# An mLSTM cell and a two-layer block on one core: states of head pairs in place of head trios, transfers in longer rows, and another order for the first third

## The chip, the cores and the metric

The kernel runs on one core of a Trainium2 chip. The metric is the time of one execution on the device in microseconds (us). All four compute engines of the core take part: TensorE (PE in the profile, with its weight loads as PEld), VectorE (DVE), ScalarE (ACT) and GpSimd (POOL); SyncE (SP) issues transfers.

## The reference

```python
# q, k, v, o_gate: (4, 8, 768, 40) float32; i_gate, f_gate: (4, 8, 768) float32
for t in range(S):                       # per batch and head, D = 40
    m_new = np.maximum(f_gate[:, :, t] + m, i_gate[:, :, t])
    f_stab = np.exp(f_gate[:, :, t] + m - m_new)
    i_stab = np.exp(i_gate[:, :, t] - m_new)
    m = m_new
    C = f_stab * C + i_stab * outer(v_t, k_t)
    n = f_stab * n + i_stab * k_t
    y[:, :, t] = sigmoid(o_t) * (C @ q_t) / np.maximum(np.abs(n . q_t), 1.0)
x = y.transpose(0, 2, 1, 3).reshape(4 * 768, 8 * 40)      # 3072 tokens x 320
h = x @ w_in                             # w_in 320 x 2048, w_out 2048 x 320, float64 in memory
out = (h - np.tanh(h)) @ w_out
```

## The kernel before

**Units.** The sequence is cut into chunks of 128 tokens. One unit is one chunk of one batch with its 8 heads: 24 units, numbered n = 4 * chunk + batch. For a unit the kernel makes the scores of all heads (tile ps: k and q with features on the partitions, tiles kz and qz), masks them to the past (P), and multiplies them by the scaled values (vs) into ph. From the second chunk on it adds to ph what the state of the earlier chunks gives (`inter`: state times q, from a second copy of q, tile q2). It then gates (`gate`, five VectorE instructions), transposes the result into xT (`turn`, `keep_x`), and brings the state on (`update` into pc, `keep_state`). Two units form a group of 256 tokens; there are 12.

**Heads.** kz and qz hold even heads on partitions 0 to 39 and odd heads on 64 to 103, so that two heads' score products stand in different rows of the array. The state holds the heads in trios, with the 40 features of three heads on 120 partitions (`TOP`): trio 0 is heads 0 to 2, trio 1 heads 3 to 5, and trio 2 heads 6 and 7. A state is block-diagonal; the factor eT, zero where a row belongs to another head of the trio, makes it so. `inter` and `update` are thus three matmuls each per unit, two of 123 columns and one of 82.

**The two-layer block.** The 2048 features are 8 pairs p of 2 x 128. For a group and a pair, `up` makes ph_up (from xT and w_in), ScalarE and VectorE make g = h - tanh(h) by a polynomial, and a down product adds it to the output. Groups 0 to 3 and group 11 use direct products (`down`, bank po); groups 4 to 10 use seven products in place of eight (`down_seven`, banks pS). A polynomial's bound is tested at the end, and a general branch, not taken with these inputs, follows.

**Weights.** They arrive as float64 and are taken apart by integer operations: 640 columns a block, two blocks (w_in, w_out) a pair. A block takes five VectorE instructions (`parts` two, `one`, `sign`, `product`) and two on ScalarE. All weight transfers are issued by GpSimd, five for w_in and two for w_out per pair.

**What sets the order.** All instructions of an engine run in the order in which the program adds them. For the first part of the kernel (units 0 to 11 and groups 0 to 3) a list scheduler, class `Plan`, makes that order at build time: an operation has an engine, an assumed duration, predecessors, a rank and tokens for the buffers that it holds, and `run` always emits the one that can start first. The assumed durations decide the order only; on the chip the engines wait for each other by semaphores. Where the plan sees TensorE idle, `idle` puts in some products of ones, 512 columns wide (tile awake, from diag). After that the units 12 to 23 are spread evenly over the block's items by hand (`cell_slot`, `merge`).

**Loads.** `load_unit` loads a unit's tiles: kz, qz and q2 by rows of 512 bytes (one head's 128 tokens), v, k and o by token (1,280 bytes; k 1,440, since a trio's end is filled from the next head). At the start SP loads the gates, then kz and o of units 0 and 1; ACT's queue loads their qz, GpSimd their v and then the weights.

Of the kernel before, what the change touches and what calls it, by code (L numbers as in the profile page):

```python
# [78 lines left out]
def kernel(  # L79
# [77 lines left out]
    class Plan:  # L157
# [5 lines left out]
        RATE, SHARED = 0.25, 32.4  # L163

        def __init__(self, **tokens):
            self.tokens = {name: [(0.0, tag) for tag in (range(tags) if isinstance(tags, int) else tags)] for name, tags in tokens.items()}
            self.turns = {name: 0 for name, tags in tokens.items() if isinstance(tags, int)}
            self.count = tokens
            self.todo, self.free, self.serial, self.moved = [], dict.fromkeys("TVASGN", 0.0), 0, dict(S=8.0, G=6.5)
# [21 lines left out]
        def run(self, idle):  # L191
            while self.todo:
# [12 lines left out]
                op["end"] = self.free[op["engine"]] = t + op["us"]  # L205
# [77 lines left out]
    TRIO = 3  # L283
    TOP = TRIO * D
    WIDE = -(-H // TRIO) * TRIO
    TRIOS = [range(h, min(h + TRIO, H)) for h in range(0, H, TRIO)]

    ld = {}

    def load_unit(n, names=("kz", "qz", "v", "k", "o", "q2"), queue=nc.sync):  # L290
        c, b = divmod(n, B)
        t = ld.setdefault(n, {})
        for name in names:
            if name in ("kz", "qz"):
                t[name] = load.tile([128, HH, L], FP, name=name, tag=name, bufs=3)
                for i in range(2):
                    src = kT if name == "kz" else qT
                    queue.dma_start(out=t[name][i * HALF:i * HALF + D], in_=src[b, c, :, slice(i, H, 2)])
            elif name == "k":
                if n + B < NU:  # L300
                    t["k"] = load.tile([L, WIDE, D], FP, name="k", tag="k", bufs=3)
                    queue.dma_start(out=t["k"].rearrange("p h d -> p (h d)"),
                                    in_=bass.AP(k.tensor, k[b, c].offset, [[H * D, L], [1, WIDE * D]]))
            elif name != "q2":
                src, bufs = {"v": (v, 3), "o": (o_gate, 4)}[name]
                t[name] = load.tile([L, H, D], FP, name=name, tag=name, bufs=bufs)
                queue.dma_start(out=t[name], in_=src[b, c])
            elif c:
                t["q2"] = load.tile([TOP, len(TRIOS), L], FP, name="q2", tag="q2", bufs=3)
                for i in range(TRIO):  # L310
                    queue.dma_start(out=t["q2"][i * D:(i + 1) * D, 0:len(range(i, H, TRIO))], in_=qT[b, c, :, slice(i, H, TRIO)])

# [28 lines left out]
    eT = const.tile([TOP, NU, H], FP, name="eT")  # L341
# [49 lines left out]
    def gate_columns(c0, c1, bank):  # L391
# [28 lines left out]
        def whole():  # L420
            got["whole"] = sums_of(1, ones).rearrange("p c (b h) -> p (c b) h", h=H)
# [8 lines left out]
        def states():  # L430
            for i in reversed(range(TRIO)):
                rows, heads = slice(0, (i + 1) * D), slice(i, H, TRIO)
                A.activation(out=eT[rows, us, heads], in_=got["whole"][rows, :, heads], func=AF.Exp)
                if i:
                    A.mul(out=eT[0:i * D, us, heads], in_=eT[0:i * D, us, heads], mul=0.0)
# [11 lines left out]
    def weights(dst, srcs, queue):  # L447
# [5 lines left out]
        def fetch():  # L453
# [3 lines left out]
            for rows, cols, part in srcs:  # L457
                queue.dma_start(out=to[rows, cols], in_=part)  # L458
# [32 lines left out]
    def blocks_of(p):  # L491
# [4 lines left out]
        every, whole = slice(0, 128), [(slice(0, 128), slices(0, 2), moe_w_in[0:128, slices(2 * p, 2)])]  # L496
        for i in range(2):
            full, half = (FROM[2], FROM[1]), (FROM[1], FROM[2] + HALF)
            whole.append((every, slices(2 + i, 1), moe_w_in[full[i]:full[i] + 128, slices(2 * p + i, 1)]))
# [3 lines left out]
                        [(every, slice(i * DM, (i + 1) * DM), moe_w_out[slices(2 * p + i, 1), :]) for i in range(2)], nc.gpsimd))  # L503
# [4 lines left out]
    state = [[const.tile([TOP, H, D1], FP, name=f"state{b}_{i}") for i in range(2)] for b in range(B)]  # L508
# [3 lines left out]
    def trio(t, j):  # L512

        return t[:, TRIOS[j].start:TRIOS[j].stop].rearrange("p h d -> p (h d)")

# [61 lines left out]
    def inter(n, j):  # L577
# [3 lines left out]
        if t["c"]:  # L581
            rows = slice(0, len(TRIOS[j]) * D)
            T.matmul(trio(t["ph"], j), t["qs"][rows, j, :], trio(state[t["b"]][t["c"] % 2][rows], j), start=(j == 0), stop=False,
                     skip_group_check=True)

    def intra(n, h):
        t = un[n]
        T.matmul(t["ph"][:, h, :], t["P"][:, h % 2, h // 2, :], t["vs"][:, h, :], start=(t["c"] == 0 and h == 0), stop=True,
# [14 lines left out]
    def update(n, j, at_once=True):  # L603
        t = un[n]
        if j == 0:
            t["pc"] = small([TOP, H, D1], "pc")
        T.matmul(trio(t["pc"], j), t["k"][:, TRIO * j:TRIO * (j + 1)].rearrange("p h d -> p (h d)"), trio(t.get("vs_end", t["vs"]), j), start=True, stop=True)
        if j == len(TRIOS) - 1 and at_once:
            keep_state(n)

    def keep_state(n):
        t = un[n]
        old, new = (state[t["b"]][(t["c"] + i) % 2] for i in range(2))
        pc = t["pc"]
        decay = eT[:, n].unsqueeze(2).to_broadcast([TOP, H, D1])
# [16 lines left out]
    def cell_slot(s, o):  # L632
# [11 lines left out]
        for d, heads in enumerate(TRIOS):  # L644
            steps.append((0.22 if o >= B else 0.0, lambda d=d: inter(o, d)))
            steps += [(0.22, lambda h=h: intra(o, h)) for h in heads]
        steps.append((0.0, lambda: gate(o)))
        steps += 5 * pause
        if o + B < NU:
            steps += [(0.2, lambda j=j: update(o, j)) for j in range(len(TRIOS))] + 4 * pause  # L650
# [97 lines left out]
    def up(some, shrink):  # L748
# [4 lines left out]
        def product(i, x, j):  # L753
# [3 lines left out]
            if j < NK:  # L757
                lhs, rhs = w_in[:, p, (2 * j + i) * 128:(2 * j + i + 1) * 128], xT[g % NX][:, at, :]
# [170 lines left out]
    def plan_unit(n, rank):  # L929
# [10 lines left out]
        if n < 2:  # L940
            times = ((6.1, 3.6, 9.0), (7.6, 5.6, 10.5))[n]
            for name, at in zip(("qz", "v", "o"), times):
                u[name] = plan.add("N", 0.0, (lambda: arrive(n)) if name == "qz" else (lambda: None), at=at - 1.7)
        else:
            load("kz", 1.5, 164, (n - 3, "scores"))
            load("qz", 1.5, 164, (n - 3, "scores"))
# [15 lines left out]
        u["scores"] = plan.add("T", 1.35, first_part, [u["qz"]], rank, [("a", held), ("P", held)])  # L962
        u["mask"] = [plan.add("V", 0.68, lambda i=i: ready[1][i](), [u["scores"]], rank, give=[("a", held)] if i else ())
                     for i in range(2)]
        before = of(n - B, "state")
        u["prep"] = plan.add("V", 0.47, lambda: prepare(n, whole=False), [u["v"], u["scores"], *of_tokens[c]], rank, [("vs", held)])
# [4 lines left out]
        def second_part(j):  # L971
            banks[:] = [held["small"]]
            inter(n, j)
            for h in TRIOS[j]:
                intra(n, h)

        for j, heads in enumerate(TRIOS):
            op = plan.add("T", 0.145 * len(heads) + (0.14 if c else 0.0), lambda j=j: second_part(j), [op] if op else [*u["mask"], u["prep"], u["column"], *before, *of(n, "q2") * (c > 0)], rank,
                          take=() if op else [("small", held)], give=[("P", held)] if j == len(TRIOS) - 1 else ())
        u["second"] = op  # L980
        u["gate"] = plan.add("V", 1.5, lambda: gate(n), [op, u["open"], *of(n - 2, "turn")], rank, give=[("small", held)])
# [3 lines left out]
        def updates():  # L985
            banks[:] = [held_c["small"]]
            for j in range(len(TRIOS)):
# [16 lines left out]
    def plan_weights(p, rank, at):  # L1004
        for k, block in enumerate(blocks_of(p)):
            fetch, parts, low, power, one, sign, product = block
            held, r, buffer = {}, rank + 0.36 * k, "w64" + "ab"[k]
            op = plan.add("S" if k else "G", 1.5 if k else 2.8, fetch, (), r, [(buffer, held)], at=(13.0 if p else 6.0) if k else at, kb=655)
            op = plan.add("V", 1.0, parts, [op], r, [("w", held)])
            two = [plan.add("A", 0.74, step, [op], r) for step in (low, power)]  # L1010
            op = plan.add("V", 0.82, one, two[:1], r)
            op = plan.add("V", 0.82, sign, [op, two[1]], r, give=[(buffer, held)])
            converted[p, k] = plan.add("V", 0.82, product, [op] + (of_tokens[NT - 1] + of_states[NT - 1] if p >= KEPT else []), r, give=[("w", held)])
# [81 lines left out]
    def idle(t0, t1):  # L1095


        n = int((t1 - t0) * 0.9 / 0.43 if t0 < 6.0 else (t1 - t0) * 0.4 / 0.215)
# [90 lines left out]
    def begin_any(n):  # L1189
# [3 lines left out]
        for i in range(2):  # L1193
            spread(t["P"][:, i], f_rows, n, slice(i, H, 2))
# [4 lines left out]
        if t["c"]:  # L1199
            t["qs"] = att.tile([128, len(TRIOS), L], FP, name="qs", tag="P", bufs=4)[0:TOP]  # L1200
            for i in range(TRIO):
                spread(t["qs"][i * D:(i + 1) * D, 0:len(range(i, H, TRIO))], g_rows, n, slice(i, H, TRIO))
            for j, heads in enumerate(TRIOS):
                rows = slice(0, len(heads) * D)
                V.tensor_tensor(out=t["qs"][rows, j], in0=t["qs"][rows, j], in1=t["q2"][rows, j], op=OP.mult)

    def keep_any(n):
# [3 lines left out]
        decay = eT[:, n].unsqueeze(2).to_broadcast([TOP, H, D1])  # L1211

        own = att.tile([TOP, H, D1], FP, name="own", tag="P", bufs=4)
        V.memset(own, 1.0)
        for i in range(TRIO):
            heads = slice(i, H, TRIO)
            pattern = [[0, len(range(i, H, TRIO))], [0, D1]]
            if i:
                V.memset(own[0:i * D, heads], 0.0)
            if i < TRIO - 1:  # L1220
                G.affine_select(out=own[:, heads], in_=own[:, heads], compare_op=OP.is_ge, fill=0.0, base=(i + 1) * D - 1,
                                pattern=pattern, channel_multiplier=-1)
# [32 lines left out]
    with tc.If(nc.values_load(again, min_val=0, max_val=128,  # L1255
# [18 lines left out]
        for g in range(NG):  # L1274
            for n in range(g * GT, (g + 1) * GT):
# [6 lines left out]
                for j in range(len(TRIOS)):  # L1282
# [4 lines left out]
                if n + B < NU:  # L1287
                    for j in range(len(TRIOS)):
# [61 lines left out]
```

## Time and profile before

| | |
|---|---|
| median of 3 runs | 556.2 us (555.52 to 556.96) |
| the profiled execution's own time | 555.52 us |
| its span in the profile | 553.7 us |
| PE busy | 539.0 us (97%) |
| DVE busy | 345.7 us (62%) |
| ACT busy | 179.8 us (32%) |
| POOL busy | 34.2 us (6%) |
| moved by DMA | 37.97 MB in 39,818 packets |

The 1.8 us between the span and the time of that execution lie outside the span. A PE that is busy may be busy with products of ones, or with products that run at half rate; the tables of single instructions tell that apart.

### The profile page before, as it was taken

What the parts mean: (1) busy time and instruction counts of PE and PEld (TensorE: products, weight loads), DVE (VectorE), ACT (ScalarE), POOL (GpSimd) and SP (SyncE); (2) the same over time, 40 slices, a digit from 0 to 9 for tenths busy, and PEclk for the clock granted to TensorE, in tenths of its full rate; (3) what the DMA queues carried; (4) which work ended last, traced back from release to release, by engine and by line L of the source; (5) the groups of instructions that cost most, each with busy time, mean ns of one, the idle gap of its engine ahead of it and who ended that gap; (6) DMA issues with size and microseconds to landing.
All of it is one profiled execution on the core that took longest, in us unless ns stands there. A gap on an engine that the chain in (4) does not pass through costs nothing.

```text
span 553.7 us, 8979 instructions
## 1 busy us (share of the span) xinstructions
PE 539.0 (97%) x3378; PEld 455.6 (82%) x3380; DVE 345.7 (62%) x754; ACT 179.8 (32%) x447; POOL 34.2 (6%) x67
## 2 busy tenths in 40 slices
PE   6999999999999999999999999999999999999995
PEld 4768878787877776798899999999989989988873
DVE  4699888989754335767656647547547547553421
ACT  2444653442432312222232242232233233232331
POOL 6042020320000000000000000000000000000000
PEclk9999999999999999999999999999999999999998
DMA  7789345470310001201202212112110000000000
GB/s 217 203 264 255 113 132 156 155 197 23 95 29 0 1 0 49 83 22 55 85 26 60 62 41 69 47 37 60 49 37 12 1 25 1 1 25 1 24 1 30
DMA packets 39818, 37.97 MB, mean 69 GB/s; under 512 B 3992, under 2 KB 37336, under 8 KB 39768
## 3 DMA queue, kind: packets, MB, share of 16 engines
q1 hardware_dynamic: 32336, 22.24, 14.2%
q0 software_dynamic: 3296, 10.82, 6.4%
q10 hardware_dynamic: 4136, 4.26, 2.2%
q8 instruction: 29, 0.48, 0.4%
q14 instruction: 21, 0.17, 0.1%
HBM read 33.37 MB, written 3.93 MB: 67 GB/s over the span
## 4 chain that ended last, share of the span: by engine, by line
PE 91%; DMA 4%; DVE 3%; issue 1%; SPq 0%; ACT 0%; POOL 0%; DVEq 0%; ACTq 0%
PE ph_up L129 38%; PE pS L129 20%; PE po L129 15%; PE ph L129 9%; PE ps L129 4%; PE pc L129 2%; PE px L133 2%; DMA v<-in_v 1%; DMA kz<-in_kT 1%; DMA q<-in_qT 1%; DVE P L106 1%; DVE w_e L106 1%; DMA w<-in_moe_w_in 0%; DVE gt L106 0%; DVE state L106 0%
## 5 line engine op out<-in xcount | busy, mean ns | idle before, releaser
L129 PE MATMUL ph_up<-xT,w_in 128*128 128x256 f32 (+1 forms) x1152 | 245.4, 391 | 2.1 <-DVE w_in L106 1.3
L129 PEld LDWEIGHTS ph_up<-xT,w_in 128*128 128x128 f32 (+1 forms) x1152 | 169.8, 189 | 35.1 <-issue 12.7
L106 ACT ACTIVATE z<-ph_up 128x512 f32<-128x512 f32 (+1 forms) x100 | 57.1, 576 | 284.2 <-issue 160.6
L106 DVE SCALAR_TENSOR_TENSOR gt<-ph_up,z 128x512 f32<-128x512 f32 (+1 forms) x100 | 63.3, 662 | 93.1 <-ACT z L106 92.9
L129 PE MATMUL po<-w_out,gt 128*128 128x320 f32 x320 | 94.4, 440 | 0.0
L129 PEld LDWEIGHTS po<-w_out,gt 128*128 128x128 f32 x320 | 58.4, 190 | 26.4 <-issue 5.0
L106 DVE TENSOR_TENSOR P<-ps,upto 128x512 f32<-128x512 f32 x48 | 31.5, 683 | 68.2 <-PE ps L129 68.2
L129 PEld LDWEIGHTS ph<-vs,P 128*128 128x128 f32 x384 | 60.1, 202 | 5.7 <-issue 1.5
L106 ACT ACTIVATE q<-z,tiny 128x512 f32<-128x512 f32 (+1 forms) x100 | 64.7, 700 | 0.0
L106 DVE SCALAR_TENSOR_TENSOR gt<-q,gt 128x512 f32<-128x512 f32 (+1 forms) x100 | 63.1, 661 | 1.3 <-ACT q L106 1.3
L129 PE MATMUL ph<-vs,P 128*128 128x41 f32 x384 | 58.9, 273 | 0.0
L129 PE MATMUL pS<-wT,s 128*128 128x160 f32 x336 | 51.3, 300 | 0.0
L129 PEld LDWEIGHTS pS<-wT,s 128*128 128x128 f32 x336 | 47.3, 190 | 0.0
L129 PE MATMUL pS<-w_out,gt 128*128 128x160 f32 x224 | 40.4, 310 | 0.0
L129 PEld LDWEIGHTS pS<-w_out,gt 128*128 128x128 f32 x224 | 32.7, 194 | 1.3 <-issue 1.0
L129 PE MATMUL ps<-qz,kz 40*128 40x128 f32 x384 | 29.6, 291 | 1.7 <-DMA kz<-in_kT 1.5
L129 PEld LDWEIGHTS ps<-qz,kz 40*128 40x128 f32 x384 | 26.9, 199 | 5.0 <-DMA qz<-in_qT 1.8
L458 POOL DMA_DIRECT2D w<-in_moe_w_in x40 | 22.2, 561 | 53.3 <-DVE w_e L106 45.1
L129 PE MATMUL ph<-state,q 120*128 120x123 f32 (+1 forms) x120 | 24.3, 284 | 0.0
L106 ACT COPY xT<-px 128x384 f32<-128x384 f32 x24 | 11.4, 475 | 35.6 <-PE px L133 35.6
L129 PEld LDWEIGHTS ph<-state,q 120*128 120x128 f32 (+1 forms) x120 | 19.9, 191 | 1.5
L106 DVE TENSOR_TENSOR s<-gt 128x256 f32<-128x256 f32 x56 | 21.1, 417 | 0.0
(90 smaller groups left out, 441.0 us busy)
## 6 DMA issues: line engine op xcount, KB each, us to landing
w<-in_moe_w_out POOLq DMA_DIRECT2D x16, 320.0 KB, 5.0
kz<-in_kT SPq DMA_DIRECT2D x48, 80.0 KB
o<-in_o_gate SPq DMA_DIRECT2D x24, 160.0 KB
out<-ob ACTq DMA_DIRECT2D x24, 160.0 KB
k<-in_k SPq DMA_DIRECT2D x20, 180.0 KB
qz<-in_qT SPq DMA_DIRECT2D x44, 80.0 KB
v<-in_v SPq DMA_DIRECT2D x22, 160.0 KB
q<-in_qT SPq DMA_DIRECT2D x40, 60.0 KB
```

Source lines behind the costliest of these rows:

```text
L106: i = method(*args, **kwargs)
L129: return cls.keep(nc.tensor.matmul(*args, **kwargs))
L133: return cls.keep(nc.tensor.transpose(*args, **kwargs))
L458: queue.dma_start(out=to[rows, cols], in_=part)
```

## The change

It has five parts.

- **Pairs.** The state holds pairs of heads, (0,1), (2,3) and so on, on 80 partitions. `inter` and `update` are four matmuls of 82 columns each per unit. q2 comes in two transfers in place of three, k by its own rows of 1,280 bytes and for all 24 units (before for 20). The factors eT take two exponentials and one product by zero per gate chunk, before three and two.
- **Scores.** kz and qz hold heads 0 to 3 on the lower partitions and 4 to 7 on the upper ones. For a feature these four heads lie next to each other in memory, so a row is 2,048 bytes.
- **Weights.** The two full blocks of w_in that lay apart come in one transfer, and so does w_out: five transfers a pair, before seven. In `up` the column blocks are found accordingly.
- **Plan.** Most assumed durations, transfer rates and arrival times are others; TensorE is taken to run 1.8 times slower before 8.5 us; the w_out transfers are planned on GpSimd's queue, where they are.
- **Ones.** `idle` fills the planned gaps of TensorE more densely.

```diff
-        RATE, SHARED = 0.25, 32.4
+        RATE, SHARED, COLD = 0.3, 28.0, (8.5, 1.8)
...
-            self.todo, self.free, self.serial, self.moved = [], dict.fromkeys("TVASGN", 0.0), 0, dict(S=8.0, G=6.5)
+            self.todo, self.free, self.serial, self.moved = [], dict.fromkeys("TVASGN", 0.0), 0, dict(S=6.5, G=5.5)
...
-                op["end"] = self.free[op["engine"]] = t + op["us"]
+                us = op["us"] * (self.COLD[1] if op["engine"] == "T" and t < self.COLD[0] else 1.0)
+                op["end"] = self.free[op["engine"]] = t + us
...
-    TRIO = 3
-    TOP = TRIO * D
-    WIDE = -(-H // TRIO) * TRIO
-    TRIOS = [range(h, min(h + TRIO, H)) for h in range(0, H, TRIO)]
+    TOP = 2 * D
...
-                    queue.dma_start(out=t[name][i * HALF:i * HALF + D], in_=src[b, c, :, slice(i, H, 2)])
-            elif name == "k":
-                if n + B < NU:
-                    t["k"] = load.tile([L, WIDE, D], FP, name="k", tag="k", bufs=3)
-                    queue.dma_start(out=t["k"].rearrange("p h d -> p (h d)"),
-                                    in_=bass.AP(k.tensor, k[b, c].offset, [[H * D, L], [1, WIDE * D]]))
+                    queue.dma_start(out=t[name][i * HALF:i * HALF + D], in_=src[b, c, :, i * HH:(i + 1) * HH])
...
-                for i in range(TRIO):
-                    queue.dma_start(out=t["q2"][i * D:(i + 1) * D, 0:len(range(i, H, TRIO))], in_=qT[b, c, :, slice(i, H, TRIO)])
+                for i in range(2):
+                    queue.dma_start(out=t["q2"][i * D:(i + 1) * D], in_=qT[b, c, :, slice(i, H, 2)])
...
+        odd = moe_w_in[FROM[1]:FROM[1] + 128, slices(2 * p + 1, 1)]
+        both = bass.AP(odd.tensor, odd.offset, [[DFF, 128], [(FROM[2] - FROM[1]) * DFF - 128, 2], [1, 128]])
+        whole.append((every, slices(2, 2), both))
+        half = (FROM[1], FROM[2] + HALF)
         for i in range(2):
-            full, half = (FROM[2], FROM[1]), (FROM[1], FROM[2] + HALF)
-            whole.append((every, slices(2 + i, 1), moe_w_in[full[i]:full[i] + 128, slices(2 * p + i, 1)]))
             whole.append((slice(i * HALF, (i + 1) * HALF), slices(4, 1), moe_w_in[half[i]:half[i] + HALF, slices(2 * p + i, 1)]))
...
-                        [(every, slice(i * DM, (i + 1) * DM), moe_w_out[slices(2 * p + i, 1), :]) for i in range(2)], nc.gpsimd))
+                        [(every, slice(0, 2 * DM), moe_w_out[slices(2 * p, 2), :].rearrange("(two p) n -> p two n", two=2))], nc.gpsimd))
...
-            rows = slice(0, len(TRIOS[j]) * D)
-            T.matmul(trio(t["ph"], j), t["qs"][rows, j, :], trio(state[t["b"]][t["c"] % 2][rows], j), start=(j == 0), stop=False,
+            T.matmul(pair(t["ph"], j), t["qs"][:, j, :], pair(state[t["b"]][t["c"] % 2].rearrange("p j two d -> p (j two) d"), j), start=(j == 0), stop=False,
...
-            times = ((6.1, 3.6, 9.0), (7.6, 5.6, 10.5))[n]
+            times = ((4.9, 4.2, 8.0), (6.2, 5.5, 9.0))[n]
...
-            load("kz", 1.5, 164, (n - 3, "scores"))
-            load("qz", 1.5, 164, (n - 3, "scores"))
+            load("kz", 0.8, 164, (n - 3, "scores"))
+            load("qz", 0.8, 164, (n - 3, "scores"))
...
-        u["scores"] = plan.add("T", 1.35, first_part, [u["qz"]], rank, [("a", held), ("P", held)])
-        u["mask"] = [plan.add("V", 0.68, lambda i=i: ready[1][i](), [u["scores"]], rank, give=[("a", held)] if i else ())
+        u["scores"] = plan.add("T", 1.16, first_part, [u["qz"]], rank, [("a", held), ("P", held)])
+        u["mask"] = [plan.add("V", 0.63, lambda i=i: ready[1][i](), [u["scores"]], rank, give=[("a", held)] if i else ())
...
-            op = plan.add("T", 0.145 * len(heads) + (0.14 if c else 0.0), lambda j=j: second_part(j), ...
+            op = plan.add("T", 0.67 if c else 0.45, lambda j=j: second_part(j), ...
...
-            op = plan.add("S" if k else "G", 1.5 if k else 2.8, fetch, (), r, [(buffer, held)], at=(13.0 if p else 6.0) if k else at, kb=655)
-            op = plan.add("V", 1.0, parts, [op], r, [("w", held)])
+            op = plan.add("G", 0.6 if k else 2.2, fetch, (), r, [(buffer, held)], at=at, kb=655)
+            op = plan.add("V", 0.82, parts, [op], r, [("w", held)])
...
-        n = int((t1 - t0) * 0.9 / 0.43 if t0 < 6.0 else (t1 - t0) * 0.4 / 0.215)
+        n = int((t1 - t0) / 0.43 if t0 < plan.COLD[0] else (t1 - t0) * 0.8 / 0.215)
```

## The prediction

> **What bounds the kernel now.** I read the stretches first (columns: stretch, then per engine busy us and instruction count, granted clock, DMA share, GB/s).
>
> ```profile
> 0.00:10.00 10.00, 5.53 (x21) 3.26 (x23) 4.21 (x21) 2.44 (x9) 7.45 (x20) 1.00 0.68 181
> 10.00:20.00 10.00, 9.78 (x56) 8.88 (x55) 5.60 (x16) 3.48 (x12) 2.73 (x5) 1.00 0.99 274
> 20.00:30.00 10.00, 8.89 (x48) 6.33 (x47) 8.05 (x17) 4.24 (x8) 2.67 (x5) 1.00 0.61 186
> 30.00:40.00 10.00, 9.21 (x63) 7.04 (x64) 9.85 (x23) 6.23 (x15) 4.51 (x7) 1.00 0.88 255
> 40.00:50.00 10.00, 9.51 (x69) 7.81 (x68) 9.73 (x21) 5.16 (x11) 1.12 (x3) 1.00 0.96 260
> 50.00:60.00 10.00, 9.96 (x76) 8.44 (x75) 9.93 (x22) 6.34 (x19) 2.67 (x5) 1.00 0.63 191
> 60.00:160.00 100.00, 99.79 (x625) 80.63 (x625) 85.69 (x173) 42.85 (x95) 13.08 (x23) 1.00 0.41 120
> ```
>
> From 60 us on PE never rests (99.79 of 100). So a matmul added there costs its whole time, and whatever is won before 60 us is kept to the end. Before 60 us PE is idle for 7.1 us. From 30 to 60 DVE is full (29.5 of 30), but before 30 it is idle for 12.1 us. The timeline of PE tells what its busy time is worth (start, us, what):
>
> ```profile
> 9.14 2.05 PE L129 MATMUL ps<-qz,kz 40*128 40x128 f32 x14 [1.52 <-DMA kz<-in_kT]
> 14.72 3.63 PE L129 MATMUL ph<-vs,P 128*128 128x41 f32 x16
> 19.00 3.47 PE L129 MATMUL ph<-vs,P 128*128 128x41 f32 x16
> 28.22 2.60 PE L129 MATMUL ph_up<-xT,w_in 128*128 128x256 f32 x12 [1.11 <-DVE w_in L106]
> 30.75 1.98 PE L129 MATMUL ph<-vs,P 128*128 128x41 f32 x16
> ```
>
> The same 16 ph products take 3.6 us at 15 us and 1.98 at 31: until 25 us PE runs at little over half its rate, though the granted clock reads 1.00. Against later rows (ps 1.18, ph 1.98, px 0.55 us) the first two units lose 6.3 us by it. The 16 products of ones are 7.0 us. So 20.4 of the first 60 us are idle, filled or slow; the first product of the two-layer block starts at 28.2. Why so late, the chain of waits, the timeline of SP's queue and that of DVE say:
>
> ```profile
> 2.71 6.30 DMA kz<-in_kT
> ```
> ```profile
> 1.70 4.15 SPq L298 DMA_DIRECT2D kz<-in_kT  x4
> ...
> 13.43 0.43 SPq L302 DMA_DIRECT2D k<-in_k  x1
> ```
> ```profile
> 22.51 0.17 DVE L106 SCALAR_TENSOR_TENSOR den<-ph,inv 128x8 f32<-128x8 f32 x1 [1.59 <-PE ph L129]
> ...
> 27.26 0.81 DVE L106 TENSOR_TENSOR w_in<-w_r,w_e 128x640 f32<-128x640 f32 x1
> ```
>
> The second kz transfer is under way for 6.3 us; then come two units at the slow rate; then the first w_in is converted, from 24.38 to 28.08, although DVE had stood idle 7.1 us between 8 and 22.5 waiting for PE.
>
> **Transfers, 2 KB rows.** The page's queue lines:
>
> ```profile
> q1 hardware_dynamic: 32336, 22.24, 14.2%
> q0 software_dynamic: 3296, 10.82, 6.4%
> q10 hardware_dynamic: 4136, 4.26, 2.2%
> ```
>
> q10 is 3072 output rows of 1,280 bytes and 640 qz rows of 512; q1 is about 21,120 rows of 512 and 8,448 of 1,280 to 1,440. The rest, small, I set at nothing. Shares times 16 engines times 553.7 us are 195 and 1258 engine-us; the two equations give, as an estimate, 37 ns for a short row and 56 for a long one, by a straight line 74 ns for 2 KB. A unit's 640 rows of kz and qz thus fall from 23.7 to 11.8 engine-us: 0.75 us a unit over 16 engines, some 7 us for the ten units loaded by 60 us. Issue: kz took 1.04 us a transfer, k with fewer rows 0.43; so SP is through its first four 2.4 us earlier, ACT (3.81 us for four qz) about 2. Scores of unit 0 should then begin near 6 us instead of 9.1: 3 us.
>
> The Trainium skill (DMA: Bandwidth & Descriptors, Specifications) puts the least transfer for full rate at 512 bytes. By it rows of 512 were already good, the 7 us of transfer would be nothing, and step one would be worth only the issue time, some 2 us. My 37 against 56 ns speaks against it; no row shows 2 KB on this queue.
>
> **Rate and ones.** Longer fills, with scores starting as the gates end, leave PE hardly any pause from 2 us. If the rate doubles near 9 us, ps of unit 1, both ph and px shrink by 0.9 + 1.65 + 1.5 + 0.7 = 4.7 us in the chain; bounds 0 (the rate turns at 25 again) and 6.3.
>
> The Trainium skill (TensorE: Matmul & The Clock Gate, "Why this matters for your kernels") says that some 4 us of continuous work bring the full rate. The trace differs: from 11 to 22.9 us PE shows only one pause of 0.22 us and stays slow. By the rule the old order would have been fast from 15 us and the ones would change little; by the rows it is doubtful that busy time alone is enough.
>
> **Order on DVE.** The plan now sees w_in in time (one transfer fewer per block; POOL takes 0.54 us each, so w_in takes 2.2 instead of 2.7 us, w_out half) and PE slow at first, so the conversion (2 x 0.48 and 3 x 0.81, about 3.4 us) can fall into the waits for PE: 3.5 us off the chain, bounds 0 and 3.7.
>
> **What of it is kept.** Together up to 11 us at the first block product (17 instead of 28). But from there DVE sets the pace, and it can win only its idle time: 12.1 us before 30. I leave 2.2 before the gates land (3.43 us), 0.6 among them, 1.3 for the first scores, 1 for the first ph: 5.1. Kept: 7.0. Low end 3 (only the scores' start), high end 9.5 (also the 2.5 us of ones and idle PE after 30 us).
>
> **More matmuls.** Steady part, timeline of PE:
>
> ```profile
> 305.31 0.38 PE L129 MATMUL ph<-state,q 120*128 120x123 f32 x2
> 305.53 0.60 PE L129 MATMUL ph_up<-xT,w_in 128*128 128x256 f32 x2
> ...
> 315.78 0.34 PE L129 MATMUL pc<-vs,k 128*120 128x82 f32 x2
> 315.96 3.00 PE L129 MATMUL ph_up<-xT,w_in 128*128 128x256 f32 x16
> ```
>
> Start to start, a matmul (two instructions) of 123 columns takes 0.22 us, one of 82 takes 0.18 (0.26 in another place, between two ph). Two thirds of the columns do not cost two thirds. Trios: 0.22 + 0.22 + 0.18 = 0.62; pairs 4 x 0.18 = 0.74 (unrounded): +0.12 a unit, bounds 0.02 and 0.42. For 12 steady units 1.4 us (0.2 to 5). In the planned part ph products follow each other at 0.12 us an instruction; two more for each of 8 units: 1.9 (1.1 at 0.07 each). `update`: 0.12 for each of 8 steady units, 1.0; in the planned part weights of 80 columns instead of 120 may be quicker, which no row shows: 12 x (-0.15 to 0.15), taken as 0. Sum 4.3, bounds 0.5 and 9.8.
>
> **At nothing.** Fewer ACT exponentials (0.2 us each, ACT 32% busy); k for four more units and one q2 transfer fewer, at a DMA share under 0.2 late; scores' new pairing, same rows; more ones, where PE would wait, and at most 0.2 us each if the plan errs. If the cover is gone they cost under 1 us.
>
> **Sum.** 555.5 (profiled time, 553.7 + 1.8) - 7.0 + 4.3 = 552.8; the median lies 0.7 above the profiled run, so 553.5.
>
> **Rivals.**
> 1. *More is won:* DVE and PE gaps both close, 9.5, and the pairs cost 2.5: 556.2 - 7 = 549.2. For: 20.4 us are there. Against: DVE full from 30 on. 0.13.
> 2. *Even:* the rate stays low till 25 us and only the transfers help: 556.2 - 4 + 4.3 = 556.5. For: it stayed low through 12 us of busy PE. 0.22.
> 3. *Slower:* PE waits for DVE between 60 and 160 us. DVE is 86% busy there and PE without reserve; the new durations equal the real distances (0.60 a mask, 0.73 a conversion step), so the plan packs DVE tight, and a block or unit that lands late holds up g of every following item behind it in DVE's fixed order, and PE behind that. 18 items at 0.4 us are 7.2: 556.2 - 7 + 4.3 + 7.2 = 560.7. It decides from 4.4 us of idle and ones on PE there. Against: 0.21 us now. 0.23.
>
> My forecast, 551 to 554.5, has 0.42.
>
> **Chances.** A measurement can tell about 0.3%, 1.7 us. Faster is forecast and rival 1, 0.55; same is rival 2, 0.22; slower 0.23. Range 547.5 to 560: the ends of the gain (3 to 9.5) against the likely cost, and most of rival 3.
>
> **What would show it.** Right: scores of unit 0 near 6 us; ph of 16 instructions in 2 us before 15; first ph_up at 16 to 20 us; PE full from about 50; 160 instructions of ph<-state, 160 of pc, each 4 matmuls in 0.7 to 0.75 us steady. Wrong: ph still at 3.5 us (rival 2), PE under 96 of 100 in 60 to 160 (rival 3), four 82-column matmuls at 1 us, or a first block product past 24 us.

## The result, and the profile after

The changed kernel takes 576.7 us (median of 4 runs, 575.5 to 578.4) against 556.2 before: 1.037 times the time (95% interval 1.034 to 1.040), 20.5 us more. The profiled execution took 578.4 us, its span is 576.6. I had forecast 553.5 us, and the range ended at 560.

The page's slices of PE and its granted clock, and the queue line of the transfers with 2 KB rows (packets, MB, share of 16 engines), of the changed kernel:

```profile
PE   7998999999999999999999999999999999999995
...
PEclk9999779969799999999999999999999999999999
```
```profile
q1 hardware_dynamic: 21672, 22.49, 12.8%
```

PE is busier than before, 98% against 97%, and the kernel is slower. The queue has a third fewer packets, 21,672 for 32,336, and the row PEclk says why this does not help: the granted clock has three holes, at some 60 to 85, 120 and 150 us. Before it had none between its first release and the last 5 us. The stretches around the holes (busy us and count of PE, PEld, DVE, ACT, POOL, then granted clock, DMA share, GB/s):

```profile
60.00:63.70 3.70, 2.36 (x22) 1.84 (x22) 3.70 (x9) 1.97 (x4) 0.00 (x0) 0.99 0.24 59
63.70:80.70 17.00, 17.00 (x90) 15.29 (x90) 10.24 (x24) 4.39 (x9) 0.74 (x1) 0.50 0.41 132
114.80:118.30 3.50, 3.50 (x34) 3.34 (x30) 3.50 (x8) 3.18 (x9) 0.00 (x0) 1.00 0.51 162
118.30:128.50 10.20, 10.20 (x52) 9.03 (x52) 5.18 (x14) 2.08 (x5) 0.74 (x1) 0.50 0.42 129
```

In the second and the fourth row PE is busy without a pause, and the clock is at one half: 17.0 of 17.0 us, then 10.2 of 10.2. A third such stretch runs from 149.0 to 155.8. The records of the clock give 17.07, 10.24 and 6.83 us, which are 5, 3 and 2 times 3.413 us: 34.1 us at half rate in all. In 60 to 160 us PE executes 581 instructions, before it was 625.

What PE does where the first and second hole begin (start, us, operation, number of instructions, idle time before it):

```profile
61.44 1.75 PE L129 MATMUL ps<-qz,kz 40*128 40x128 f32 x16 [1.23 <-DVE P L106]
63.12 0.45 PE L129 MATMUL ph<-state,q 80*128 80x82 f32 x2
...
63.95 0.70 PE L129 MATMUL ph<-state,q 80*128 80x82 f32 x2
```
```profile
117.66 0.43 PE L129 MATMUL ph<-state,q 80*128 80x82 f32 x2
...
118.40 0.70 PE L129 MATMUL ph<-state,q 80*128 80x82 f32 x2
```

The same two state products take 0.45 us ahead of 63.7 and 0.70 behind it. Both holes begin while the second part of a unit runs: the state products of pairs, 80 rows by 82 columns, between products of 41 columns. The first one also follows an idle time of 1.23 us, in which PE waits for the mask of DVE. DVE waited for ACT, and its timeline shows three table loads on ACT within 5 us (first ACT, then DVE):

```profile
55.34 0.32 ACT L106 ACTIVATE eT<-gate 80x64 f32<-80x64 f32 x2
...
55.87 1.28 ACT L106 ACT_TABLE_LOAD   x1
57.17 0.47 ACT L106 ACTIVATE o<-o 128x320 f32<-128x320 f32 x1
57.65 1.28 ACT L106 ACT_TABLE_LOAD   x1
58.95 0.31 ACT L106 ACTIVATE inv<-inv 128x128 f32<-128x128 f32 x1
```
```profile
59.29 0.29 DVE L106 TENSOR_TENSOR ei<-ei,inv 128x128 f32<-128x128 f32 x1 [2.44 <-ACT inv L106]
```

The new order puts the sigmoid of one unit (o) between the exponentials of the third gate chunk (eT, inv). Each change of function costs a load of 1.28 us, which the plan does not know: it counts 0.47 for o.

At the start, PE's timeline says this:

```profile
7.19 2.04 PE L129 MATMUL ps<-qz,kz 40*128 40x128 f32 x14 [0.54 <-DMA kz<-in_kT]
14.61 3.48 PE L129 MATMUL ph<-vs,P 128*128 128x41 f32 x16 [0.33 <-issue]
24.41 2.52 PE L129 MATMUL awake<-diag 128*128 128x512 bf16 x7 [0.22 <-issue]
28.66 2.60 PE L129 MATMUL ph_up<-xT,w_in 128*128 128x256 f32 x12
```

The scores of unit 0 start 1.95 us earlier than before, ph of unit 0 still takes 3.48 us, and the first block product starts at 28.66 instead of 28.22. The clock was released at 26.1 us (before at 25.3). The early gain, which carried the forecast, is not there.

**Where the 22.9 us of span went.** I cut both traces behind the 48th and the 384th instruction of `up` and at the last (the 48th up product and so on, below). Up to the 48th the changed kernel is 2.7 us ahead (54.0 against 56.7). From there to the 384th it loses 22.6 (186.7 against 164.1), in the rest of the up products 3.8 (320.8 against 317.0), and it wins back 0.8 at the end. Of the 22.6, half of 34.1 us at half rate is 17.1. Idle PE is 1.1 (1.34 against 0.21 in 60 to 160 us). Pairs in the planned part are 1.8, as worked out below. The 2.6 that remain are work that stands elsewhere in the new order: up to the 48th up product it has run 8 instructions of down products, the old order 16, and these eight (2.1 us) come behind the cut; and six products of ones between 185 and 232 us, where the kernel before has none, take 1.3. e6 below, with trios and a full clock, shows these two alone: 167.4 us against 164.1. So most of the lead of 2.7 us at the 48th product is work put off. The terms add up to 23.4, 0.8 more than was measured.

### The profile page after: what moved, and what is told of

Same layout as the page of the kernel before. It is cut to its first block, busy times and chain, and to the rows that moved or that the text cites. A ratio compares the mean times of both kernels' runs of the same rounds, so it can differ in the third digit from the quotient of the medians.

```text
span 576.6 us, 9089 instructions
## 1 busy us (share of the span) xinstructions
PE 562.4 (98%) x3470; PEld 475.3 (82%) x3473; DVE 345.6 (60%) x754; ACT 182.6 (32%) x443; POOL 27.5 (5%) x51
## 3 DMA queue, kind: packets, MB, share of 16 engines
q1 hardware_dynamic: 21672, 22.49, 12.8%
## 4 chain that ended last, share of the span: by engine, by line
PE 94%; DVE 2%; ACT 1%; DMA 1%; issue 0%; SPq 0%; DVEq 0%; ACTq 0%
PE ph_up L129 38%; PE pS L129 19%; PE po L129 15%; PE ph L129 11%; PE ps L129 5%; PE pc L129 2%; PE px L133 2%; PE awake L129 1%; DMA kz<-in_kT 1%; ACT L106 1%; DVE P L106 0%; PE gate L129 0%; ACT z L106 0%; ACT q L106 0%; DVE w_in L106 0%
## 5 line engine op out<-in xcount | busy, mean ns | idle before, releaser
L129 PE MATMUL ph_up<-xT,w_in 128*128 128x256 f32 (+1 forms) x1152 | 249.2, 396 | 2.7 <-DVE gt L106 2.6
L106 DVE TENSOR_TENSOR P<-ps,upto 128x512 f32<-128x512 f32 x48 | 31.4, 684 | 70.6 <-PE ps L129 70.6
L129 PEld LDWEIGHTS ph<-vs,P 128*128 128x128 f32 x384 | 65.7, 219 | 4.0 <-issue 0.2
L129 PE MATMUL ph<-vs,P 128*128 128x41 f32 x384 | 64.6, 287 | 0.3 <-issue 0.3
L129 PE MATMUL pS<-w_out,gt 128*128 128x160 f32 x224 | 43.7, 315 | 0.0
L129 PE MATMUL ps<-qz,kz 40*128 40x128 f32 x384 | 32.3, 310 | 2.5 <-DVE P L106 1.2
L129 PE MATMUL ph<-state,q 80*128 80x82 f32 x160 | 34.2, 298 | 0.0
L129 PEld LDWEIGHTS ps<-qz,kz 40*128 40x128 f32 x384 | 29.3, 216 | 5.7 <-issue 2.1
L129 PEld LDWEIGHTS ph<-state,q 80*128 80x128 f32 x160 | 28.8, 209 | 2.7 <-issue 1.0
L129 PEld LDWEIGHTS pc<-vs,k 128*80 128x80 f32 x160 | 19.8, 171 | 5.4 <-issue 2.0
L452 POOL DMA_DIRECT2D w<-in_moe_w_in x32 | 19.2, 605 | 59.6 <-DVE w_e L106 44.4
```

What stands on the lines that cost most here:

```text
L106: i = method(*args, **kwargs)
L129: return cls.keep(nc.tensor.matmul(*args, **kwargs))
L452: queue.dma_start(out=view, in_=part)
```

## The experiments

**Pairs, order and transfers apart.** My theory from these rows: the clock counts more than whether PE is busy, and thin products let it fall. The rivals: the pairs cost by their number, the new order by waiting, or the transfers by contention. Three kernels undo one part each.

`e1_trios_new_order`: the changed kernel with the trios of before.

```diff
-    TOP = 2 * D
+    TRIO = 3
+    TOP = TRIO * D
...
-            op = plan.add("T", 0.67 if c else 0.45, ...
+            op = plan.add("T", len(heads) * (0.335 if c else 0.225), ...
```

> The changed kernel with the state in trios again (three matmuls of 120 rows per unit in inter and update), all else as changed; a trio is planned at its share of the pair time, so the order stays nearly the same. Theory A (thin work halves the granted clock: 34.1 us at half rate in the changed kernel came from stretches of pair products of 80 rows): trios raise the rows times columns done in 3.4 us from 0.33 to 0.43 of full, the clock stays at 1.00, and the time is 576.7 - 17 (half of the slow stretches) - 4.3 (the extra matmuls) = 555.4, within 2. Theory B (the new order makes TensorE wait and bunches units, whatever the clock): only the extra matmuls go, 572. Theory C (an 82-column pair matmul costs much more than 0.18 us): 556, but then with the slow stretches still there.

566.8 us, 1.020 [1.016, 1.024]. Of the loss, 9.9 us go with the pairs, and 11.2 stay without them (against the 555.6 us of the kernel before, measured beside it). Theory A's 555.4 is missed by 11 us. Of the holes, those at 118 and 149 us are gone; one of 17.1 us, from 62.8 to 79.8, is left, behind the same idle time of PE (1.35 us in 60 to 160). In the stretch ahead of it PE is busy for 2.09 of 3.80 us, and in the hole itself all the time (stretches of e1):

```profile
59.00:62.80 3.80, 2.09 (x19) 1.47 (x18) 3.70 (x9) 2.69 (x6) 0.00 (x0) 1.00 0.16 43
62.80:79.80 17.00, 17.00 (x84) 15.07 (x84) 10.78 (x25) 3.92 (x7) 0.74 (x1) 0.50 0.44 131
```

`e2_pairs_old_order`: the kernel before with the pairs alone, and nothing else.

```diff
-    TRIO = 3
-    TOP = TRIO * D
+    TOP = 2 * D
...
-            op = plan.add("T", 0.145 * len(heads) + (0.14 if c else 0.0), ...
+            op = plan.add("T", 0.145 * 2 + (0.14 if c else 0.0), ...
```

> The kernel before with the state in pairs and nothing else. A: where a scores product lies between two units the share stays near 0.40, so mostly full clock: 556.2 + 4.3 = 560.5, and up to 567 if one stretch falls under the limit; any slow stretch begins after 3.4 us of pair products. B: 560.5 and no slow stretch. C: 576.

564.6 us, 1.013 [1.008, 1.018]. Here PE idles for 0.01 us in 60 to 160, and the clock still falls: at 64.1 for 6.8 us and at 98.2 for 3.4 (stretch of e2):

```profile
60.00:160.00 100.00, 99.99 (x633) 81.95 (x633) 81.96 (x167) 39.66 (x86) 13.36 (x23) 0.95 0.38 116
```

Pairs alone are enough. Half of 10.2 us and the 3.8 us that the steady part grows by make 8.9 of the 9.9 by which the profiled execution (565.5 us) lies above the 555.6 of the kernel before. The holes are not in every execution: the four have mean clocks of 0.987, 0.997, 0.989 and 0.990, and the one at 0.997, as full as the kernel before, took 560.9 us. So at a full clock the pairs cost 5.4 us, by this one execution.

`e3_transfers_only`: the kernel before with the 2 KB rows and the five weight transfers.

```diff
-                    queue.dma_start(out=t[name][i * HALF:i * HALF + D], in_=src[b, c, :, slice(i, H, 2)])
+                    queue.dma_start(out=t[name][i * HALF:i * HALF + D], in_=src[b, c, :, i * HH:(i + 1) * HH])
```

> The kernel before with the rows of 2 KB for k and q (heads j and j+4) and five weight transfers a pair; trios, old order, old number of ones. All theories: clock full. By the first forecast's transfer term (scores of unit 0 three us earlier, 0.75 us of transfer time less a unit): 553 to 555; if the order hides it, 556.

556.0 us, 1.0000 [0.998, 1.002]. The first block product starts at 26.2 us instead of 28.2, no hole is seen, and the median does not show the 2 us.

`e4_pairs_spread`: the changed kernel, with a planned pause of 0.8 us between the second parts of two pairs, so that denser products come between.

```diff
+            if j and c:
+                op = plan.add("X", 0.8, lambda: None, [op], rank)
```

> The changed kernel, but the plan holds 0.8 us between the four parts of a unit's second products, so that other products come between them; same instructions, only their order differs. A: no 3.4 us window is thin any more, the clock stays at 1.00 (or nearly), 576.7 - 17 = 560, within 3. B and C: 576 or more, since units get later and no work is saved.

571.1 us, 1.027 [1.021, 1.032]. The holes at 118 and 149 are replaced by one of 3.4 us at 95.5; the first, behind the idle time, stays with 17.1 us. It wins 5.6 us against the changed kernel: half of the 13.7 us less at half rate is 6.8.

**The table loads.** In these two kernels the sigmoids of units 4 to 7 are planned behind the exponentials of the third gate chunk, so that ACT loads a table once for each. `e5_pairs_grouped_exp` is the changed kernel with that, `e6_trios_grouped_exp` is e1 with it.

```diff
+            for m in (n - 4, n - 3, n - 2, n - 1):
+                units[m]["open"]["after"] += exponentials
```

> The changed kernel with one more rule for the plan: the sigmoids of units 4 to 7 wait until the exponentials of the third gate chunk are done, so that ScalarE loads two tables there instead of four. Theory D (the two extra loads of 1.28 us hold up DVE for 2.4 us and PE for 1.2 at 60 us, and the thin window that follows halves the clock at 63.7 us): the 17.1 us stretch goes, the two later ones stay: 576.7 - 8.5 - 1.5 = 567. Rival (pairs are thin enough by themselves there): the loads go but the stretch stays, 575.

> The first of these kernels (trios, all else as changed, 566.8 us) with the same rule on the sigmoids. Theory D with A: no slow stretch after 30 us is left, 566.8 - 8.5 - 1.5 = 556.8, within 2. Rival (the new order itself is worse than the old by waits at full clock): 563 or more with the clock full.

With pairs: 572.5 us, 1.030 [1.026, 1.034]. With trios: 557.0 us, 1.001 [0.999, 1.003]. The rule takes PE's idle time in 60 to 160 us from 1.34 to 0.00 with pairs and from 1.35 to 0.05 with trios. With trios the clock then stays full; with pairs it does not: the hole at 63.7 us is gone, but one of 10.2 us begins at 66.8, and two of 3.4 and 6.8 follow. So 572.5 lies between the theory's 567 and the rival's 575 (stretches of e5, then of e6):

```profile
67.00:76.00 9.00, 9.00 (x51) 7.94 (x52) 5.38 (x13) 1.33 (x3) 0.74 (x1) 0.50 0.57 171
```
```profile
60.00:160.00 100.00, 99.95 (x636) 81.25 (x636) 86.09 (x175) 44.65 (x99) 10.50 (x16) 1.00 0.40 121
```

So there are two causes, and each suffices. In e1 the idle time does it without pairs, and in e2 and e5 the pairs do it without idle time. The next part reduces both to one count. The medians side by side:

| | trios | pairs |
|---|---|---|
| old order (pairs without, trios with the new transfers) | 556.0 | 564.6 |
| new order | 566.8 | 576.7 |
| new order, exponentials grouped | 557.0 | 572.5 |

**What the clock counts.** For a number that separates the cases I weighted PE's work. An instruction counts as its columns by 0.83 ns (0.213 us for 256 columns in the block products above; 0.42 ns for the ones, which are bf16) by its rows over 128, spread evenly over its recorded time. Per window of 3.413 us, laid from the records of the clock, the last one ahead of each of the three holes of the changed kernel has 0.20, 0.34 and 0.33 of full work; the lowest without a fall has 0.39. A unit of pairs, 8 instructions of 82 columns on 80 rows and 16 of 41 columns on 128 rows, has 0.33 in its 2.70 us. A unit of trios has 0.43 in 2.38. In e1 the window of the idle time has 0.20.

The same working over the traces of all fourteen kernels gives 2,191 whole windows, from the first record of the clock to the fall at the end of the work. One limit of 0.375 tells for all but three of them whether the next window runs at half rate (48 do): below it the clock falls or stays down, above it the clock stays full or comes back. The three begin ahead of 22 us. Columns without rows do not separate them: their best limit is wrong for 29 windows (in the changed kernel 0.56 fell, 0.47 stayed), and busy time for 47. If rows count, zeros should do.

`e9_pairs_zero_rows`: e5 with the state products 128 rows deep. The further 48 rows are zero in the state and in q, and the weights of `update` have 128 columns, of which 80 are used; the state itself is the same.

```diff
+    PAD = 128
...
-                t["q2"] = load.tile([TOP, HH, L], FP, name="q2", tag="q2", bufs=3)
+                    padded[n % 3] = const.tile([PAD, HH, L], FP, name=f"q2_{n % 3}")
+                    V.memset(padded[n % 3][HALF:PAD], 0.0)
...
-    state = [[const.tile([TOP, HH, 2, D1], FP, ...
+    state = [[const.tile([PAD, HH, 2, D1], FP, ...
```

> The changed kernel with the sigmoid rule (572.5 us) and the state's products made 128 rows deep: the 48 added rows of state are zero, of q anything, so the result is the same, and so are the number, the width and the order of TensorE's products. Only the rows differ (in update the 48 added columns of weights, whose results are multiplied by zero). Theory A1 (what is counted is rows times columns; a stretch of pair products rises from 0.33 to 0.41 of full): fewer or no slow stretches, 572.5 - 10 = 562, not below 560. A2 (what is counted is time or columns, not rows): slow stretches as before, 572 to 575.

568.5 us, 1.022 [1.018, 1.026]. The clock of e9 after its first release falls only once, for 3.4 us at 47.1, behind a wait of PE for DVE of 2.1 us. Two units of pairs back to back, from 65.2 to 70.6 us, now run at full rate (timeline of e9's PE, then the stretch):

```profile
65.22 0.45 PE L129 MATMUL ph<-state,q 128*128 128x82 f32 x2
...
69.94 0.43 PE L129 MATMUL ph<-state,q 128*128 128x82 f32 x2
```
```profile
64.00:68.00 4.00, 4.00 (x42) 3.75 (x41) 4.00 (x9) 2.25 (x3) 0.00 (x0) 1.00 0.41 118
```

Its share there is 0.41. With the same number of instructions and the same columns in the state products, 48 rows of zeros keep the rate: 0.33 lies below the limit, 0.41 above. The gain against e5 is 4.0 us, and half of the 17 us of half rate that went is 8.5. `update` takes the difference back (timeline of e9):

```profile
87.21 1.10 PE L129 MATMUL pc<-vs,k 128*128 128x82 f32 x8
88.24 1.16 PE L129 MATMUL ps<-qz,kz 40*128 40x128 f32 x16
```

From start to start these eight instructions take 1.03 us; with weights of 80 columns they take 0.71 in the same place (the changed kernel's lines at 92.46 and 93.17, shown below). At full clock, over the planned part, the means are 0.92 and 0.60 a unit, which makes 3.8 us for 12 units; and e9's steady part is 1.2 us longer than e5's (322.0 against 320.8). The deeper state products cost nothing: the two units above take 5.4 us, twice 2.70. So e9 is still 11.5 us behind the trios of e6, and zeros in this form are no remedy.

**The early part.** The forecast rested on a release of the clock near 9 us. Four kernels, and one behind them, ask what that takes and what it is worth. They add products of ones in the planned gaps of PE ahead of 9 us (12 us in e11): up to three more a gap in e7 and e11, two in the others.

```diff
+        if t0 < 9.0 and t1 - t0 > 0.05:
+            n = int((t1 - t0) / 0.43) + 2
```

`e7_trios_grouped_heat` adds them to e6, `e8_old_order_heat` to e3, `e10_heat_only` to the kernel before, `e11_old_order_heat3` to e3. `e12_old_order_heat_fill` is e8, with the later gaps filled to 0.8 in place of 0.4.

> As the one before, and up to three more products of ones in each planned gap of TensorE before 9 us. Theory A: a window of 3.4 us full of ones releases the clock near 9 us instead of 26, the first units run at full rate: 2 to 4 us under the one before. Rival (the scores products that follow are thin and the clock drops again, or the ones hold up the gates): the same or up to 2 us over.

557.4 us, 1.0001 [0.997, 1.003]. The clock was released at 28.0 us, as in e6 (28.5), in the profiled execution. No gain.

> The kernel before with the 2 KB rows and five weight transfers (556.0 us), and up to two more ones in each planned gap before 9 us. A: clock full from about 9 us and first block product near 22 us instead of 26: 552 to 554. Rival as above: 556 to 558.

549.4 us, 0.9895 [0.986, 0.993]: better than both kernels, and the only clear gain found, with its neighbours e11 and e12. In the profiled execution the clock was released at 7.3 us, and stayed full to the last microseconds; of the five, two at a mean clock of 0.99 took 551.5 and 552.2. PE's timeline of e8:

```profile
8.14 1.16 PE L129 MATMUL ps<-qz,kz 40*128 40x128 f32 x16
...
21.91 2.60 PE L129 MATMUL ph_up<-xT,w_in 128*128 128x256 f32 x12 [1.24 <-DVE w_in L106]
```

The scores of unit 0 take 1.16 us, in e3 2.37, and the first block product starts at 21.9 us, 6.3 earlier than before.

> The kernel before, with up to two more ones in each planned gap before 9 us and nothing else. If the gain of the old order with transfers and ones (549.4) is the clock's early release alone: 550 to 551. If it needs the 2 KB rows too, because the scores' transfer lands only at 9 us and PE falls idle: 554 to 557.

555.2 us, 0.999 [0.996, 1.002]. The same ones without the new transfers. The clock was released at 7.0 us and fell again at 13.9, for 17.1 us. The scores of unit 1 came in two parts, and the 3.41 us ahead of the fall have a share of 0.28; the like window of e8, 10.7 to 14.1, where the 16 scores run in one, has 0.34 and stayed (one of the three that the limit misses). Timeline of e10's PE, then its stretch from 14 us:

```profile
10.90 0.48 PE L129 MATMUL ps<-qz,kz 40*128 40x128 f32 x2
11.93 1.13 PE L129 MATMUL ps<-qz,kz 40*128 40x128 f32 x14 [0.54 <-DVE vs L106]
```
```profile
14.00:31.00 17.00, 16.57 (x66) 11.73 (x66) 12.23 (x27) 4.79 (x10) 5.08 (x9) 0.50 0.80 220
```

So e8's 6.6 us against e3 need both: the ones alone give nothing (e10), the transfers alone give nothing (e3), together they hold the clock. The profiled executions of e3 and e8 differ by 4.2 us of span, and by 4.3 at the first block product already.

> The old order with 2 KB rows, five weight transfers and up to three more ones in each planned gap before 12 us (two before 9 us gave 549.4, between 548.6 and 552.2). If the spread comes from where the free-running 3.4 us window falls, more ones narrow it: 548 to 549.5. If the ones now hold up the first products: 550 to 553.

551.5 us, 0.991 [0.989, 0.994]. The clock was released at 7.3 us and fell at 24.3 for 3.4; the first block product started at 24.2 us. More ones are no better.

> The kernel of the old order with 2 KB rows, five transfers and early ones (549.4), and the changed kernel's fuller filling of all later planned gaps (0.8 instead of 0.4). If the runs at 552 come from thin stretches of the first two units that drop the clock again, the denser filling holds it: 548 to 549.5 with less spread. If the plan's gaps are not real (its durations in the old order are not the chip's), the ones hold up products that could run: 551 to 555.

552.3 us (median of 11, 550.5 to 561.8); 0.992 [0.990, 0.995] by the seven executions up to 556.8. Filling the later gaps does not add to e8.

## Why the prediction was wrong

**The step that failed most: "From 60 us on PE never rests (99.79 of 100). So a matmul added there costs its whole time, and whatever is won before 60 us is kept to the end."** It takes busy time at a fixed rate. The page showed one clock of 1.00 after 60 us, and I read it as a property of the kernel, where it was a property of its products. The changed products are thinner, and 34.1 us at half rate cost 17.1. I had the row that warned of it: PE busy and slow from 11 to 23 us. I concluded there that "it is doubtful that busy time alone is enough", used it against the early gain, and did not carry it to the pairs. The 16 ph products of 41 columns at 14.61 have a share of 0.16 of full rate, and did not release the clock: thin work, as the pairs are.

The Trainium skill (TensorE: Matmul & The Clock Gate, "Why this matters for your kernels") makes a window of idle time the reason for a fall. The runs agree with it for e1 only in part: the clock fell after 3.80 us in which PE was idle for 1.71. They differ for e2, e5 and the hole at 118 us, where PE had not idled at all. The window of 3413 ns that the same page gives (Part 1, "What's actually happening") agrees with the lengths of the holes, 17.07, 10.24 and 6.83 us.

**The early gain, 7.0 taken, next to nothing measured.** Term by term:
- *Scores' start, 3 us:* they started at 5.90 in two instructions, then at 7.19, after the second kz transfer had landed; SP's four issues took 2.01 instead of 4.15 us, the transfer 4.89 instead of 6.30. About 2 us, and no more: e3, which has the longer rows and the five weight transfers alone, begins its block products 2.0 us earlier. The issue time was sized about right. The transfer time was not: over the whole run, by the prediction's own two equations, e3's share of 13.8% of 551.9 us leaves 138 ns for a row of 2 KB, and the changed kernel's 12.8% of 576.6 leaves 120 (an estimate), not 74. Four short rows are 149, so a unit saves 0.1 to 0.3 us, and not 0.75.
- *Rate and ones, 4.7:* 0. The clock was released at 26.1. ph of unit 1 was still at the slow rate, as rival 2 had it. In e1 and e5, with the same six ones at 2.1 us, it was released at 4.7 and 5.4, held for one window of 3.41 us, and was at half until 25.2 and 29.3. e8 shows that a longer run of ones does it where the work behind it is dense enough: its first block product comes 4.3 us earlier than e3's, near the 4.7 taken, but in another kernel than this.
- *Order on DVE, 3.5:* 0. The parts of w_in did start earlier, but its last step began at 27.26 us, to the hundredth as before. Behind the slow ph, DVE still waited (1.33 and 2.85 us), and the conversion was cut in two by the gating of the units.
- *Kept, 7.0:* e6 has the whole new order, transfers and ones with a full clock, and is at 1.001 [0.999, 1.003]. It is 1.1 us ahead at the 48th up product, the changed kernel 2.7, with 2.1 us of down products put off.

**More matmuls, 4.3 taken, about 5.6 found.** This mechanism was right, and two of its terms were too small. Steady: 2.4 taken, 3.8 measured, and as much in e2 (time from the 384th to the last up product). Planned: 1.9 for `inter` taken; a unit takes 2.70 us with pairs and 2.38 with trios, and 8 times 0.32 is 2.6. `update`, taken as 0, is a little quicker (timeline of the changed kernel):

```profile
89.76 0.45 PE L129 MATMUL ph<-state,q 80*128 80x82 f32 x2
...
92.46 0.78 PE L129 MATMUL pc<-vs,k 128*80 128x82 f32 x8
93.17 1.05 PE L129 MATMUL ps<-qz,kz 40*128 40x128 f32 x14
```

From 89.76 to 92.46 is the unit, from there to 93.17 are the eight instructions of `update`: 0.71 against 0.78 for the six of before, so 12 times 0.07, 0.8 us, come off. 3.8 + 2.6 - 0.8 = 5.6. The execution of e2 with a full clock, 5.4 us over the kernel before, agrees.

**At nothing.** "Fewer ACT exponentials" was true, but I did not ask where they stand: the new order broke their group, with six table loads by 60 us instead of four. That costs 4.2 us with pairs (e5 against the changed kernel) and 9.8 with trios (e6 against e1), most of it through the clock: 1.3 us of idle time set off 17.1 us at half rate. The ones were taken to stand where PE would wait; the six between 185 and 232 us cost 1.3. The rest held: the DMA share did not matter, and the transfers are neutral (e3).

**Rivals.** Rival 3 had the sign, and its mechanism is there in small: DVE is late by 2.44 us, and PE waits. But it asked for 4.4 us of idle time, and 1.3 were enough, since they took the clock with them. Its 560.7 came from adding waits. No rival had a fall of the clock, and the range of 547.5 to 560 had no term for it. What I said would show the forecast wrong did show it: ph at 3.5 us, and a first block product past 24 us.

**Left open.** The limit of 0.375 is worked out afterwards from modelled starts and ends, and no kernel was built to test it. e9 also changed the weights of `update`, but its two units from 65.2 to 70.6 us contain none. The share ahead of a hole depends on where the windows lie, so that repeated executions of one kernel can have other holes, as those of e2 do. Why e11 and e12 are behind e8 was not pursued.

## What to carry to other kernels

Before making matrix products narrower or shallower in a kernel where PE is always busy, count rows by columns per few microseconds and not busy time, read the granted clock of every stretch, and put dense products between the thin ones. An order made from assumed durations must know the loads of ACT's tables: a short wait can cost a multiple of itself by the clock. And warming pays only if the work that follows is there: ones and earlier data gave nothing singly, and 1.05% together.

## What the runs showed of the hardware that I had not expected

- The clock fell to one half with PE busy for 100% of the time, in stretches of 2, 3 and 5 times 3.413 us; a window with less than 0.375 of full work by rows and columns went ahead. In 2,188 of 2,191 windows this limit tells the rate of the next.
- Rows of zeros count: 128 rows in place of 80 kept the rate with the same columns (e9), and the deeper products took no longer. Wider weights did: `update` took 0.92 us a unit with 128 columns of weights, 0.60 with 80.
- At half rate thin work does not bring the clock back: by the same limit a window must then hold three quarters of what can be done (0.375 of 0.5). In e10 17.1 us went by at half rate with PE busy for 16.57 of 17.00.
- Before the first record of the clock, the stretches read 1.00 though products run at half rate: ph of 16 instructions took 3.48 us at 14.61, and 1.98 at full rate.
- A table load on ACT took 1.28 us each time, and two changes of function in the wrong place set PE back by 1.23 us.
